# Eagle recurrence followed by a mixture-of-depths MLP on one core: the per-batch second part rescheduled, and the tables and first keys of the start-up rebuilt

## The chip, the cores and the metric

The kernel runs on one core of a Trainium2 chip. The metric is device time in microseconds (us) of one execution, as the median of the timed runs; before the change it is 264.77 us (three runs, 262.55 to 264.99).

## What is computed

The first part is a linear recurrence with decay, for 4 batches, 8 heads, 768 tokens and head width 48, all float32:

```
for t in range(S):
    cur = einsum('bhd,bhe->bhde', u * k[t], v[t])
    y[t] = einsum('bhd,bhde->bhe', r[t], state + cur)
    state = w * state + einsum('bhd,bhe->bhde', k[t], v[t])
```

The heads are laid side by side (8 x 48 = 384 channels) and each batch goes through the second part: every token gets a score, the 128 tokens with the highest scores of the batch go through a two-layer MLP (384 to 1024 to 384), weighted by a sigmoid of the score, and all other rows pass unchanged:

```
scores = x @ w_gate
top_idx = the 128 tokens of the batch with the highest scores
h = maximum(x[b, top_idx] @ w1, 0);  ye = h @ w2
out[b, top_idx] = x[b, top_idx] + sigmoid(scores)[:, None] * ye
```

## The kernel before

**Units.** A unit is 128 tokens of one batch with all 8 heads: 6 units in a batch (NC), 24 in all (NU). Inside a unit there are two chunks of 64 tokens. The order of instructions is written by hand (a manual schedule): each engine executes its own in the order in which the program issues them, so the place of a call in the loop is its place in the queues of all the engines that it uses.

**Tables, before the loop.** `wp` holds the powers w^(2^i) (L123 to L125), `up` and `dn` are rising and falling powers made by doubling (L131 to L142). `kt` (L144 to L147) scales keys, `tr` (L153 to L155) scales receptances; each takes one RECIPROCAL of 128x128. `kt` is transposed on the tensor engine into `wk` (L148 to L152), which scales the keys in their loaded layout. Masks and identity come from an int32 iota on POOL.

**One unit n, in the order of the loop (L459 to L489).** `load(n+4)` puts three transfers on SP's queue. `inner(n)`: 32 instructions at L237 (scores of keys and receptances) and 32 at L244 (key by value), into the one PSUM tile `rp`. `masked(n)` (L250, DVE) copies the causal part of `rp` into `AT[n]`. `state(n, 0)`: `g` on DVE (L255), then four scalings `z` on ACT (L258). `turn(n+1)`: eight transposes on the tensor engine (L216, L219) and the copy `kh` on ACT (L221); `turned(n+1)`: `rh` on DVE (L226); `bonus_sum(n+1)`: `du` on DVE (L206). POOL gets `scaled(n+2)` (`kw`, L196), `diagonal(n+1)` (`at`, L210) and `bonus(n+2)` (`rk`, `rku`, L200, L202). Then `outer(n-1)`: 64 instructions into `y` and `yx` (L272 to L284) and two copies `e` on ACT (L289); `state(n, 1)`; `finish(n-1)`: `x` (L297) and the scores `scr` (L298) on DVE, and the store of the unit.

**The second part of batch b** is hung on the ends of later units by `plan` (L432): with n = 6(b+1), unit n gets `scores_along` (six transposes at L318, two copies `srow` at L319), units n+1 and n+2 get three `compare` each (L326 `gt`, L328 equality), unit n+2 also `rank` (L333 to L341), `pick` (`oh` L350, L353, `idx` L357) and `fetch` (gather of the chosen rows, POOL, L365), unit n+3 `chosen` (transposes L381, copy `xt` L383), `gates` (L388, L391) and the first half of `hidden` (24 instructions at L399), n+4 its second half, n+5 all of `expert` (16 at L408) and `leave` (`ot` L414, scatter on POOL L416). For the last batch all of them come after the loop, in this order. PSUM tiles named `m` (two buffers) serve all of the second part.

**Start.** Before the loop the order is `scaled(0)`, `tables()` (POOL memsets of `rpads` 2 to 4, `zt`, `es`), `bonus(0)`, `bonus_sum(0)`, `turn(0)`, `turned(0)`, `load(2)`, `load(3)`, `scaled(1)`, `diagonal(0)`, `bonus(1)`. `rpads` and `kws` are cleared whole by POOL memsets.

Of the kernel before, what the change touches and what calls it, by code (L numbers as in the profile page):

```python
# [17 lines left out]
def kernel(  # L18
# [71 lines left out]
    for i in range(2):  # L90
        nc.gpsimd.memset(rpads[i], 0.0)
# [17 lines left out]
    jp = const.tile([128, 128], I32)  # L109
    nc.gpsimd.iota(jp, pattern=[[1, 128]], base=0, channel_multiplier=-1)  # L110
# [18 lines left out]


    up = const.tile([128, NP, MID + 1], F32)  # L131
    dn = const.tile([128, NP, MID + 1], F32)
    nc.vector.memset(up[:, :, 0:1], 1.0)
    nc.vector.memset(dn[:, :, MID : MID + 1], 1.0)
    h = 1
    for i in range(NW):
        n = min(h, MID + 1 - h)
        if n > 0:
            nc.vector.tensor_mul(dn[:, :, MID + 1 - h - n : MID + 1 - h],
                                 dn[:, :, MID + 1 - n : MID + 1], power(i, n))  # L140
            nc.vector.tensor_mul(up[:, :, h : h + n], up[:, :, :n], power(i, n))
        h *= 2  # L142
# [70 lines left out]
    def turn(n):  # L213
        pk = psum.tile([128, NP, T], F32, name="pk")
        for hp in range(NP):
            nc.tensor.transpose(pk[:, hp, :], kws[n % 3][:, 2 * hp : 2 * hp + 2, :], ident)  # L216
# [310 lines left out]
```

## Time and profile before

| what | value |
|---|---|
| median of the timed runs | 264.77 us (262.55 to 264.99) |
| the profiled execution's own time | 261.97 us |
| its span, first to last instruction | 260.2 us |
| mean granted clock of the tensor engine, share of 2.4 GHz | 0.821 |
| busy: PE / DVE / ACT / POOL | 178.9 / 127.8 / 85.4 / 114.1 us |

The span is what the views of the trace cover; the time of an execution is 1.77 us longer in the profiled one. An engine's busy share is an average over the start, 24 units and the tail, and no engine is busy throughout, so the limits are read unit by unit. The start of `masked(n)` on DVE serves as the mark of unit n below.

### The profile page before, as it was taken

Reading aid. Unit: us, or ns where it says so; the run is one execution under the profiler, and the core shown is the slowest. Engines: PE = TensorE matmul, PEld = TensorE weight load, DVE = VectorE, ACT = ScalarE, POOL = GpSimd, SP = SyncE. Lnnn points to the kernel's source line nnn. Section 1 sums busy time; section 2 is a strip of 40 time slices with the busy share of each in tenths; the row PEclk is TensorE's granted clock in tenths of the full one; section 3 lists DMA queues with packets and bytes.
Section 4 is the critical chain, followed back from the end, with each engine's and each line's share of the span. In section 5 each row is a group of like instructions: output and inputs, shape, how many; then the busy total and the mean of one; then the engine's idle time right before and its main releaser. Section 6 shows DMA issues by size and latency. Waiting matters only on the chain.

```text
span 260.2 us, 8407 instructions
## 1 busy us (share of the span) xinstructions
PE 178.9 (69%) x3608; PEld 153.8 (59%) x3608; DVE 127.8 (49%) x340; ACT 85.4 (33%) x274; POOL 114.1 (44%) x131
## 2 busy tenths in 40 slices
PE   0347958779609799959509799959229799721991
PEld 0236847759508698649408698659128797411970
DVE  4835765573884235353983245256873153282000
ACT  1003654552242545063232345064313253100110
POOL 4397995594443616464343526474345110101001
PEclk9999997995955799995955799988955599955699
DMA  7899498986741505532741505543001001101000
GB/s 140 133 175 130 113 373 214 193 198 138 151 95 33 121 5 123 121 99 58 149 96 33 123 7 124 119 123 92 3 33 30 33 3 46 49 33 30 0 0 30
DMA packets 81428, 24.52 MB, mean 94 GB/s; under 512 B 76272, under 2 KB 80624, under 8 KB 81392
## 3 DMA queue, kind: packets, MB, share of 16 engines
q1 hardware_dynamic: 79776, 22.03, 39.1%
q0 software_dynamic: 512, 1.57, 1.9%
q10 hardware_dynamic: 1104, 0.40, 0.8%
q8 instruction: 28, 0.46, 0.7%
q14 instruction: 8, 0.07, 0.1%
HBM read 18.48 MB, written 5.51 MB: 92 GB/s over the span
## 4 chain that ended last, share of the span: by engine, by line
PE 51%; DVE 19%; issue 11%; ACT 9%; DMA 4%; POOL 2%; SPq 1%; POOLq 0%; DVEq 0%; ACTq 0%
PE m L399 8%; PE y L272 8%; PE m L408 6%; PE rp L237 6%; PE pk L216 6%; PE rp L244 5%; DVE gt L326 5%; PE pr L219 5%; ACT e L289 4%; ACT z L258 3%; DVE scr L328 3%; DVE scr L298 3%; PE y L281 3%; DMA kin<-in_k_dram 3%; DVE x L297 3%
## 5 line engine op out<-in xcount | busy, mean ns | idle before, releaser
L258 ACT ACTIVATE z<-g,wp 128x48 f32<-128x48 f32 x176 | 44.5, 323 | 89.8 <-DVE g L255 89.3
L210 POOL TENSOR_TENSOR at<-dia,du 128x512 f32<-128x512 f32 x24 | 25.0, 1042 | 72.5 <-DVE du L206 72.4
L272 PE MATMUL y<-vin,at 64*64 64x48 f32 x768 | 42.2, 239 | 1.8 <-issue 1.8
L250 DVE COPY_PREDICATED at<-mask,rp 128x512 f32<-128x512 uint32 x24 | 17.6, 731 | 48.7 <-PE rp L244 36.6
L272 PEld LDWEIGHTS y<-vin,at 64*64 64x64 f32 x768 | 35.6, 153 | 7.5 <-issue 5.8
L284 PE MATMUL yx<-z,rh 48*64 48x48 f32 x352 | 33.1, 251 | 3.2 <-issue 3.2
L281 PE MATMUL y<-z,rh 48*64 48x48 f32 x352 | 30.6, 233 | 0.0
L297 DVE TENSOR_TENSOR x<-y,e 128x384 f32<-128x384 f32 x24 | 13.4, 558 | 33.8 <-ACT e L289 33.8
L196 POOL TENSOR_TENSOR kw<-kin,wk 128x384 f32<-128x384 f32 x24 | 25.2, 1052 | 10.3 <-DVE wk L152 7.5
L399 PE MATMUL m<-xt,w 128*128 128x128 f32 x192 | 29.2, 322 | 0.0
L399 PEld LDWEIGHTS m<-xt,w 128*128 128x128 f32 x192 | 28.2, 236 | 0.2
L202 POOL TENSOR_TENSOR rku<-rk,ub 128x384 f32<-128x384 f32 x24 | 26.8, 1115 | 1.9
L237 PE MATMUL rp<-rh,kh 48*64 48x64 f32 x768 | 20.5, 255 | 7.1 <-DVE rh L226 3.7
L281 PEld LDWEIGHTS y<-z,rh 48*64 48x64 f32 x352 | 22.5, 150 | 2.8 <-issue 2.8
L200 POOL TENSOR_TENSOR rk<-rpad,kin 128x384 f32<-128x384 f32 x24 | 24.0, 1002 | 0.2 <-DMA rpad<-in_r_dram 0.2
L237 PEld LDWEIGHTS rp<-rh,kh 48*64 48x64 f32 x768 | 17.0, 162 | 10.8 <-issue 5.9
L289 ACT COPY e<-yx 64x192 f32<-64x192 f32 x48 | 15.0, 313 | 23.5 <-PE y L281 15.8
L408 PE MATMUL m<-w,ht 128*128 128x384 f32 x64 | 21.6, 491 | 0.0
L216 PE MATMUL pk<-ident,kw 128*128 128x128 f32 x96 | 20.3, 347 | 1.8 <-POOL kw L196 1.8
L336 PE MATMUL m<-ones,gt 128*128 128x1 bf16 x60 | 4.6, 169 | 23.8 <-DVE gt L326 23.8
L284 PEld LDWEIGHTS yx<-z,rh 48*64 48x64 f32 x352 | 20.6, 143 | 0.6 <-issue 0.6
L244 PE MATMUL rp<-vin,kw 64*64 64x48 f32 x704 | 20.2, 247 | 0.3
(81 smaller groups left out, 288.3 us busy)
## 6 DMA issues: line engine op xcount, KB each, us to landing
kin<-in_k_dram SPq DMA_DIRECT2D x24, 192.0 KB, 4.0
rpad<-in_r_dram SPq DMA_DIRECT2D x24, 192.0 KB, 4.1
vin<-in_v_dram SPq DMA_DIRECT2D x24, 192.0 KB, 3.5
out_dram<-x SPq DMA_DIRECT2D x24, 192.0 KB, 2.0
w<-in_moe_w_dram SPq DMA_DIRECT2D x2, 1536.0 KB, 10.4
ub<-in_u_dram ACTq DMA_DIRECT2D x1, 192.0 KB, 4.8
wg<-in_moe_w_gate_dram ACTq DMA_DIRECT2D x1, 192.0 KB, 5.4
xr<-out_dram,idx POOLq DMA_INDIRECT x4, 3.2
```

The source lines that it names most:

```text
L196: nc.gpsimd.tensor_mul(kws[n % 3][:, :, :D], KIN[n], wk)
L202: nc.gpsimd.tensor_mul(RKU[n], rk, ub)
L216: nc.tensor.transpose(pk[:, hp, :], kws[n % 3][:, 2 * hp : 2 * hp + 2, :], ident)
L237: nc.tensor.matmul(out=rp[ts, i, hp * C : (hp + 1) * C], lhsT=KH[n][rows, hp, ts], rhs=RH[n][rows, hp, ts], start=True, stop=True)
L244: nc.tensor.matmul(out=rp[i * PAD : (i + 1) * PAD, c, NP * C + hp * D : NP * C + (hp + 1) * D], lhsT=kws[n % 3][ts, 2 * hp + i, :], rhs=VI ...
L258: nc.scalar.activation(to[:, hp, :], g[:, hp, :], AF.Copy, scale=wc[:, hp : hp + 1])
L272: nc.tensor.matmul(out=y[ts, 2 * hp + i, :], lhsT=AT[n][ts, i * NP + hp, :], rhs=VIN[n][ts, 2 * hp + i, :], start=(hp == 0 and i == 0), st ...
L281: nc.tensor.matmul(out=y[ts, 2 * hp + i, :], lhsT=RH[n][rows, hp, ts], rhs=z[rows, hp, :], start=False, stop=True, skip_group_check=True)
L284: nc.tensor.matmul(out=yx[ts, hp, :], lhsT=RH[n][rows, hp, ts], rhs=z[rows, hp, :], start=True, stop=True)
L289: nc.scalar.copy(e[ts, :, 1 - c, :], yx[ts])
L399: nc.tensor.matmul(out=ph[:, f, :], lhsT=w1[:, d, (f0 + f) * 128 : (f0 + f + 1) * 128], rhs=XT[b, z][:, d, :], start=(d == 0), stop=(d == ...
L408: nc.tensor.matmul(out=pe[:, :Dm], lhsT=HT[b, z][:, f, :], rhs=w2[:, f, :], start=(f == 0), stop=(f == FB - 1))
```

## The change

The second part is cut into smaller steps that run one unit after the data which they read. `work_at(n, "turn")` runs steps after `bonus(n+2)` and ahead of `outer(n-1)`, `work_at(n, "end")` at the unit's end. `scores_along` moves to unit n+1, the compares to the ends of n+1 to n+3 (short ones first), `rank` and the new `match` (the `oh` half of `pick`) to n+4, `pick` and `fetch` to n+5, `chosen`, `gates` and the MLP to n+7 and after, two MLP parts to a place (`hidden` and `expert` now take two blocks at a call). For batch 2 the MLP, and for batch 3 what needs its last two units, come after the loop, interleaved; batch 3's first four units are compared in unit 23. In the start, unit 0's keys are transposed unscaled from a padded tile `k0` and scaled by `kt` on leaving PSUM (DVE), `wk` is made by `key_table` with copies on ACT, the two RECIPROCALs of 128x128 become one of 128x4 and two multiplications, memsets clear only the padding, the iota is float32, and `tables()` moves behind `bonus(1)`.

```diff
+    k0 = const.tile([128, H, PAD], F32)
...
-        KIN[n] = work.tile([128, H, D], F32, name="kin", bufs=NIN)
+        KIN[n] = work.tile([128, H, D], F32, name="kin", bufs=NIN) if n else k0[:, :, :D]
...
-    for i in range(2):
-        nc.gpsimd.memset(rpads[i], 0.0)
+    for x in [k0] + rpads[:2]:
+        nc.gpsimd.memset(x[:, :, D:], 0.0)
...
-    jp = const.tile([128, 128], I32)
+    jp = const.tile([128, 128], F32)
...
-        nc.gpsimd.memset(kws[i], 0.0)
+        nc.gpsimd.memset(kws[i][:, :, D:], 0.0)
...
     for i in range(NW - 1):
         nc.vector.tensor_mul(wp[:, i + 1, :], wp[:, i, :], wp[:, i, :])
+        h = 1 << i
+        if h < MID:
+            nc.vector.tensor_mul(dn[:, :, MID - 2 * h : MID - h], dn[:, :, MID - h :], power(i, h))
+            nc.vector.tensor_mul(up[:, :, h : 2 * h], up[:, :, :h], power(i, h))
+    back = const.tile([128, NP], F32)
+    nc.vector.reciprocal(back, wp[:, MID.bit_length() - 1, :])
+    back = back[:, :, None].to_broadcast([128, NP, MID])
+    nc.vector.tensor_mul(kt[:, :, 0, MID:], dn, back)
+    nc.vector.tensor_mul(tr[:, :, :MID], up, back)
...
-    nc.vector.reciprocal(kt[:, :, 0, MID:], up[:, :, 1:])
-    nc.vector.tensor_copy(kt[:, :, 1, :], kt[:, :, 0, :])
...
-    nc.vector.tensor_copy(wk, p.rearrange("s p (i d) -> s (p i) d", i=2)[:, :, :D])
...
-    nc.vector.reciprocal(tr[:, :, :MID], dn[:, :, :MID])
+    def key_table():
+        nc.scalar.copy(kt[:, :, 1, :], kt[:, :, 0, :])
+        p = psum.tile([128, NP, 128], F32, name="m", bufs=2)
+        for hp in range(NP):
+            nc.tensor.transpose(p[:, hp, :], kt[:, hp, :, :], ident)
+        nc.scalar.copy(wk, p.rearrange("s p (i d) -> s (p i) d", i=2)[:, :, :D])
...
-            nc.gpsimd.memset(rpads[i], 0.0)
+            nc.gpsimd.memset(rpads[i][:, :, D:], 0.0)
...
-        nc.scalar.copy(KH[n], pk)
+        if keys is not None:
+            nc.vector.tensor_mul(KH[n].rearrange("d p (c t) -> d p c t", c=2),
+                                 pk.rearrange("d p (c t) -> d p c t", c=2),
+                                 kt[:, :, 0:1, :].to_broadcast([128, NP, 2, C]))
+        else:
+            nc.scalar.copy(KH[n], pk)
...
-    def compare(b, c):
+    def compare(b, c, first, last):
         s = sc[b][:, c : c + 1]
...
+        lo = max(c, first)
+        nc.vector.tensor_scalar(GT[b][:, c, lo:last, :], SR[b][:, lo:last, :], s, None, op0=OP.is_gt, op1=OP.add,
+                                accum_out=RS[b][-1][:, c : c + 1])
+        if first <= c:
+            nc.vector.scalar_tensor_tensor(scr[:, :128], SR[b][:, c, :], s, earlier, op0=OP.is_equal, op1=OP.mult,
+                                           accum_out=ES[b][:, c : c + 1])
+    def count(b):
+        q = ES[b]
+        for rs in RS[b]:
+            to = work.tile([128, NC], F32, name="q", bufs=4)
+            nc.vector.tensor_add(to, rs, q)
+            q = to
+        QQ[b] = q
...
-        ph = psum.tile([128, 4, 128], F32, name="m", bufs=2)
-        for f in range(4):
+        if f0 % 4 == 0:
+            PH[b, z] = psum.tile([128, 4, 128], F32, name="m", bufs=2)
+        ph = PH[b, z]
+        for f in range(f0, f0 + 2):
...
-        nc.scalar.activation(HT[b, z][:, f0 : f0 + 4, :], ph, AF.Relu)
+        if f0 % 4 == 2:
+            nc.scalar.activation(HT[b, z][:, f0 - 2 : f0 + 2, :], ph, AF.Relu)
...
+    def mlp(b, z):
+        for f0 in range(0, FB, 2):
+            yield hidden, (b, z, f0)
+        for f0 in range(0, FB, 2):
+            yield expert, (b, z, f0)
+        yield leave, (b, z)
     def plan(b):
         n = (b + 1) * NC
...
+        step(n + 1, "turn", scores_along, b, 0, NC)
+        for c in range(NC):
+            step(n + 1 + c // 2, "end", compare, b, NC - 1 - c, 0, NC)
+        step(n + 3, "end", count, b)
+        step(n + 4, "turn", rank, b)
         for z in range(NST):
...
+            step(n + 4, "end", match, b, z)
+            step(n + 5, "turn", pick, b, z)
+            step(n + 5, "turn", fetch, b, z)
+        if n + 6 < NU:
+            for z in range(NST):
+                step(n + 7, "turn", chosen, b, z)
+                step(n + 7, "turn", gates, b, z)
+            parts = [p for z in range(NST) for p in mlp(b, z)]
+            per = -(-len(parts) // 8)
+            for i, (f, a) in enumerate(parts):
+                step(n + 7 + i // per // 2, ("turn", "end")[i // per % 2], f, *a)
...
+    last = B - 1
+    known = NC - 2
+    step(NU - 1, "turn", scores_along, last, 0, known)
+    for c in range(known):
+        step(NU - 1, "end", compare, last, c, 0, known)
...
-    scaled(0)
-    tables()
     bonus(0)
-    bonus_sum(0)
-    pr = turn(0)
+    pr = turn(0, k0)
+    key_table()
     turned(0, pr)
     load(2)
     load(3)
+    scaled(0)
     scaled(1)
+    bonus_sum(0)
     diagonal(0)
     bonus(1)
+    tables()
...
+        work_at(n, "turn")
         if n:
             outer(n - 1)
...
-        for f, a in fill.get(n, []):
-            f(*a)
+        work_at(n, "end")
...
     outer(NU - 1)
     finish(NU - 1)
...
+    rest = []
+    for z in range(NST):
+        chosen(last - 1, z)
+        gates(last - 1, z)
+        rest += mlp(last - 1, z)
...
+    some(2)
+    scores_along(last, known, NC)
+    for c in range(NC):
+        compare(last, c, known, NC)
+    count(last)
+    some(2)
+    rank(last)
+    for z in range(NST):
+        match(last, z)
+    some(2)
+    for z in range(NST):
+        pick(last, z)
+        fetch(last, z)
+    some(len(rest))
+    for z in range(NST):
+        chosen(last, z)
+        gates(last, z)
+        for f, a in mlp(last, z):
+            f(*a)
```

`some(k)` takes the next k parts of batch 2's MLP (`rest`).

## Rows read from the trace of the kernel before

**Rows 1.** Busy time by stretch (PE, PEld, DVE, ACT, POOL), clock, DMA share, GB/s.

```profile
30.52:35.04 4.52, 3.54 (x137) 3.27 (x136) 3.67 (x11) 3.13 (x11) 4.17 (x5) 1.00 1.00 331
25.13:53.22 28.09, 21.99 (x671) 19.84 (x671) 17.90 (x38) 14.84 (x51) 21.23 (x24) 0.94 0.79 216
53.22:216.91 163.69, 122.73 (x2562) 107.37 (x2561) 85.42 (x222) 61.20 (x198) 74.35 (x77) 0.78 0.37 84
216.91:260.20 43.29, 25.14 (x240) 18.87 (x234) 11.22 (x38) 4.96 (x14) 3.15 (x5) 0.79 0.07 24
```

**Rows 2.** Timeline of DVE, end of unit 2 and mark of unit 3.

```profile
33.72 0.56 DVE L297 TENSOR_TENSOR x<-y,e 128x384 f32<-128x384 f32 x1 [0.80 <-ACT e L289]
34.31 0.80 DVE L298 SCALAR_TENSOR_TENSOR scr<-x,wg 128x384 f32<-128x384 f32 x1
35.04 0.73 DVE L250 COPY_PREDICATED at<-mask,rp 128x512 f32<-128x512 uint32 x1
```

**Rows 3.** Timeline of ACT in the same unit.

```profile
32.55 0.59 ACT L221 COPY kh<-pk 128x512 f32<-128x512 f32 x1
33.03 0.65 ACT L289 COPY e<-yx 64x192 f32<-64x192 f32 x2
```

**Rows 4.** Busy time of a unit at the lower clock, same columns as rows 1.

```profile
58.36:64.57 6.21, 6.21 (x135) 5.79 (x138) 2.39 (x5) 1.85 (x6) 2.37 (x4) 0.50 0.71 152
```

**Rows 5.** Chain of waits in the tail: start, length, what.

```profile
230.20 0.80 DVE gt L326 x2
231.00 0.27 DVE scr L328 x2
...
233.02 0.40 DVE gt L326 x2
...
234.74 0.97 DVE oh L350
...
236.55 3.06 DMA xr<-out_dram,idx
```

**Rows 6.** Groups of instructions by form: the score copies on ACT.

```profile
L319 ACT COPY srow<-m 128x512 f32<-128x512 f32 x4 | 2.3, 586 | 0.1
L319 ACT COPY srow<-m 128x256 f32<-128x256 f32 x4 | 1.5, 373 | 1.7 <-PE m L318 1.6
```

**Rows 7.** Timeline of PE: the MLP of batch 1.

```profile
146.04 0.97 PE L388 MATMUL m<-wgc,xt 128*128 128x1 f32 x6 [1.89 <-ACT xt L383]
146.88 4.41 PE L399 MATMUL m<-xt,w 128*128 128x128 f32 x24
...
154.85 2.94 PE L399 MATMUL m<-xt,w 128*128 128x128 f32 x24
...
161.34 5.43 PE L408 MATMUL m<-w,ht 128*128 128x384 f32 x16
```

**Rows 8.** Timeline of the start, all engines.

```profile
7.72 0.94 DVE L146 RECIPROCAL kt<-up 128x128 f32<-128x128 f32 x1
...
9.04 1.11 PE L151 MATMUL m<-ident,kt 128*128 128x128 f32 x4 [9.04 <-DVE kt L147]
...
10.90 0.99 POOL L196 TENSOR_TENSOR kw<-kin,wk 128x384 f32<-128x384 f32 x1 [7.49 <-DVE wk L152]
...
11.66 2.59 DVE L160 TENSOR_SCALAR mask<-jc 128x64 f32<-128x64 int32 x1
...
13.23 0.26 POOL L177 MEMSET zt<- 128x192 f32 x1
...
13.43 0.78 POOL L179 MEMSET e<- 128x384 f32 x2
...
20.31 0.35 DVE L255 TENSOR_TENSOR g<-rp,zt 128x192 f32<-128x192 f32 x1
...
23.05 1.13 PE L237 MATMUL rp<-rh,kh 48*64 48x64 f32 x32 [1.60 <-DVE g L255]
```

**Rows 9.** Timeline of the end, last MLP's result.

```profile
254.81 0.62 DVE L414 SCALAR_TENSOR_TENSOR ot<-m,gate,xr 128x384 f32<-128x384 f32 x1 [18.54 <-PE m L408]
```

More of the change, by code (lines that the diff above doesn't have):

```diff
@@ L125 @@
         nc.vector.tensor_mul(wp[:, i + 1, :], wp[:, i, :], wp[:, i, :])
-    def power(i, n):
-        return wp[:, i, :, None].to_broadcast([128, NP, n])
[L131 to L142, printed above, removed]
@@ L305, in finish, with scores_along @@
         stores.setdefault(b, []).append(st)
-    SR, GT, RS, ES, QQ, XR, XT, IDX, GA, HT, PE = {}, {}, {}, {}, {}, {}, {}, {}, {}, {}, {}
+    SR, GT, RS, ES, QQ, XR, XT, IDX, GA, HT, PH, PE, OH = ({} for _ in range(13))
     spacer = const.tile([1, 1], F32)
     out_rows = out.rearrange("b s d -> (b s) d")
-    def scores_along(b):
-        SR[b] = work.tile([128, NC, 128], F32, name="srow")
-        for c0 in range(0, NC, 4):
-            c1 = min(c0 + 4, NC)
+    def scores_along(b, first, last):
+        if first == 0:
+            SR[b] = work.tile([128, NC, 128], F32, name="srow")
+            GT[b] = work.tile([128, NC, NC, 128], BF16, name="gt", bufs=1)
+            ES[b] = work.tile([128, NC], F32, name="eq")
+            RS[b] = []
+        for c0 in range(first, last, 4):
+            c1 = min(c0 + 4, last)
             p = psum.tile([128, 4, 128], F32, name="m", bufs=2)
@@ L406, in expert @@
         pe = PE[b, z]
-        for f in range(f0, f0 + 4):
+        for f in range(f0, f0 + 2):
             nc.tensor.matmul(out=pe[:, :Dm], lhsT=HT[b, z][:, f, :], rhs=w2[:, f, :],
@@ L430, with step, work_at @@
     fill = {}
+    def step(n, where, f, *a):
+        fill.setdefault((n, where), []).append((f, a))
+    def mlp(b, z):
[4 more added lines that the diff above has]
+        yield leave, (b, z)
     def plan(b):
         n = (b + 1) * NC
-        steps = [(n, scores_along, (b,))]
-        steps += [(n + 1 + c // 3, compare, (b, c)) for c in range(NC)]
-        steps.append((n + 2, rank, (b,)))
-        for z in range(NST):
-            steps += [(n + 2, pick, (b, z)), (n + 2, fetch, (b, z)), (n + 3, chosen, (b, z)), (n + 3, gates, (b, z))]
-            steps += [(n + 3 + f0 // 4, hidden, (b, z, f0)) for f0 in range(0, FB, 4)]
-            steps += [(n + 5 + f0 // 8, expert, (b, z, f0)) for f0 in range(0, FB, 4)]
-            steps += [(n + 5, leave, (b, z))]
-        for m, f, a in steps:
-            fill.setdefault(min(m, NU), []).append((f, a))
-    for b in range(B):
-        plan(b)
-    scaled(0)
-    tables()
+        step(n + 1, "turn", scores_along, b, 0, NC)
[3 more added lines that the diff above has]
+        step(n + 4, "turn", rank, b)
+        for z in range(NST):
+            step(n + 4, "end", match, b, z)
[9 more added lines that the diff above has]
+                step(n + 7 + i // per // 2, ("turn", "end")[i // per % 2], f, *a)
+    for b in range(B - 2, -1, -1):
+        plan(b)
+    last = B - 1
[3 more added lines that the diff above has]
+        step(NU - 1, "end", compare, last, c, 0, known)
+    def work_at(n, where):
+        for f, a in fill.get((n, where), []):
+            f(*a)
     bonus(0)
-    bonus_sum(0)
-    pr = turn(0)
+    pr = turn(0, k0)
+    key_table()
     turned(0, pr)
```

69 lines of the change are left out of this document (34 added, 35 removed).

## The prediction

> **What bounds the kernel now.** I read the busy times by stretch first, with the start of masked(n) on DVE as mark, because no engine is busy throughout. From mark 1 to mark 6, which is almost without second part, five units take 28.09 us; from mark 6 to mark 23, where the second parts of batches 0 to 2 lie, seventeen take 163.69; from mark 23 to the end 43.29 [rows 1]. So a unit costs 5.6 without and 9.6 with the second part, and PE is busy for only 122.73 of the 163.69.
>
> A unit in the open takes 4.52 us at 2.4 GHz, with PE busy for 3.54 of it [rows 1]. The timelines of DVE and ACT say what closes it: `x` waits for the `e` copies, `scr` ends as the next mark begins (34.31 + 0.80 against 35.04), and `e` comes behind `kh` in ACT's queue [rows 2, 3]. The loop is at, g, z, kh, e, x, scr, at; with 0.73, 0.59, 0.65, 0.56 and 0.73 to 0.80 for the ones in the rows, some 1.2 are left for g and z. Two rules follow. What is put on DVE behind `scr`, or on ACT between `kh` and `e`, lengthens a unit by its full duration. PE has about 1.0 us to spare; beyond that it binds (of its 3.54 I count 1.1 for inner, 1.0 for turn, 1.4 for outer). At 1.2 GHz PE is itself the bound: 6.21 us, all of it busy [rows 4].
>
> **The start.** Now the chain runs through the RECIPROCAL of `kt` (0.94), its copy, four transposes (9.04 to 10.15), `wk`, `kw` at 10.90 and POOL's memsets, which end at 14.21 [rows 8]; the first `g` comes at 20.31 and unit 1 begins on PE at 23.05. After the change what stands ahead of the RECIPROCAL (7.72) is shorter by two small multiplications and a copy (0.3), and a four-column reciprocal and one multiplication take its place (0.4, by its 0.94 for 128 columns an upper estimate): `kt` is ready at 7.9 instead of 8.7. Then ACT's copy (no row of this one; the 128x256 copy from PSUM takes 0.37 [rows 6]; 0.4) 8.3, transposes 1.11 9.4, the second ACT copy (0.55, between those of 256 and 512 columns) 10.0. POOL then has five operations of about 1.05 (kw of units 0 and 1, at 0, rk and rku 1; 0.99 for the first [rows 8]): 15.3. bonus(0) lies ahead of them in the 7.49 in which POOL now waits. Behind them comes tables(): three small memsets (at most 0.26 each by the `zt` row; 0.5 together) and `zt` itself: 16.1. That is what becomes late: the first `g` reads `zt`, so it starts at 16.2, whatever masked(0) does before, and on DVE `rh` and `du` of unit 1 are queued behind it, on ACT z and kh. From `g` to unit 1 on PE it was 2.74; with the transposes of unit 1 long done only z (1.0), kh (0.6) and latencies stay, 2.0: 18.2 instead of 23.05, **-4.8 us**. Upper end -6.0 (`kt` by 7.3, the interleaved doubling having no stall; the POOL operations as short as 0.99). Lower end -2.7: bonus(0) now runs beside the table building, two operations of 1.05 each, and if each stops DVE entirely, `kt` is 2.1 late. That engines do stop each other is in the rows: the `mask` operation on DVE stands for 2.59 us and ends at 14.25, right after POOL's last memset at 14.21 [rows 8]. I take none of the 2.1, because these rows are a one-input DVE operation against writes, and keep it in the range.
>
> The Trainium skill, "SBUF — State Buffer", section "Who interferes with whom", speaks against the change here: a DVE instruction with two SBUF inputs contends with a POOL instruction that reads SBUF, and the later one blocks until the first is through. The table multiplications are of that kind and so are rk and rku. By that rule the gain is the lower end, and the sum below 2.1 us longer; no row of the start shows the pair.
>
> Mark 1 so moves from 25.13 to 20.3; marks 1 to 6 keep their 28.1 (nothing in them changes; SP's loads are issued as early or earlier, `load(2)` no longer waits for the whole memset, and a third transfer still waits for outer(n-1)), so mark 6 is at 48.4.
>
> **The loop.** Removed are PE's waits in order: for the scores just made, for the compares ahead of rank, for `oh`, for the gathered rows; each is now read a unit later. The transfers keep their order on SP's queue and are hidden: 84 GB/s over 163.69 us become 108 over 127, where marks 1 to 6 had 216 [rows 1]. The work itself stays, by the two rules. A `gt` of 640 columns takes 0.80 in its chain, one of 256 0.40, so 0.13 for each 128 columns; each equality 0.27; `oh` 0.97 [rows 5]. At 2.4 GHz:
> - unit 6: nothing, 4.5.
> - unit 7: two srow copies between kh and e, 0.59 + 0.37 [rows 6], compares of 128 and 256 columns 0.27 + 0.40 + 0.54: 4.5 + 2.1 = 6.6.
> - unit 8: 0.53 + 0.67 + 0.54: 6.2.
> - unit 9: 0.80 + 0.93 + 0.54 and count 0.2: 7.0.
> - unit 10: rank's add and `oh`: 5.6. Rank's sixteen small matmuls fit in PE's spare 1.0.
> - unit 11: idx 0.2: 4.7. The gather adds 1.0 on POOL, which is busy 4.17 of 4.52 [rows 1]: it starts the next units up to 0.8 late, and what it makes is needed more than a unit later.
> - unit 12: 4.5.
>
> The MLP is nominally spread, but nine parts by two fill two and a half units: 13, 14 and `leave` in 15. Unit 13: in PE's order scores_along of the next batch, then `chosen`, must wait for kh and both srow copies before `xt`, and outer(12) with e, x and scr is queued behind on PE; with 1.0 for at and g, 1.0 for z, 0.6 kh, 1.0 srow, 0.3 transposes and 0.5 `xt` the gates start at 4.3 to 4.4 after the mark, take 0.97, then 24 hidden 2.94, outer 1.4, 24 hidden 2.94 and inner 1.1 [rows 7]: 13.6. Its compares lie beside PE. Unit 14: turn 1.0, expert 5.43 in two halves, outer 1.4, inner 1.1: 9.0, the compares again covered. Unit 15: `ot` falls into DVE's wait for `e`; compares and count as in unit 9: 7.0. Units 16 to 18: 5.6, 4.7, 4.5. Units 19 to 22 like 13 to 16: 35.2.
>
> Sum of marks 6 to 23: 39.1 + 44.4 + 35.2 = **118.7 us at 2.4 GHz**.
>
> **The clock.** After the stretches without matmuls the trace has 1.2 GHz: hidden's first half takes 4.41, the second 2.94 [rows 7]. A compare unit of 7.0 leaves PE idle for 3.4 of it, so I expect the fall to stay, shorter. Within compare units it costs nearly nothing: 6.21 is below 7.0. After them I charge one open unit per batch with 6.21 - 4.52 = 1.7 and a little, 2.0, and the first half of hidden 1.47: 3 x 2.0 + 2 x 1.47, less as batch 2 is cut short, 8.3. Loop: **127 us** against 163.69. Ends: 0 and 20 (below).
>
> **The tail.** From mark 23: scr(22) at 4.5, four compares 2.95, x and scr of unit 23 1.4: 8.9. Beside this PE does outer(23), chosen, gates and half of batch 2's hidden, to 10.3: it holds the last two score transposes. Copy 11.3, compares of the last two units' columns (five of 0.40, one 0.27, two equalities) 14.1, count and rank 14.9, `oh` 15.9. PE then is still in half of expert to 17.3; pick and idx 17.9, gather 3.06 and 0.3: 21.2; chosen, xt, gates 2.3: 23.5; hidden 5.9, expert 5.4: 34.8; from `ot` to the span's end 5.4 as now (254.81 to 260.2 [rows 9]): 40.2, with 1.4 for a cold half of hidden 41.6 against 43.29. So the tail gives little: batch 2's MLP now lies in it.
>
> **Sum.** 20.3 + 28.1 + 127 + 41.6 = 217.0 us of span, with the 1.77 outside it 218.8 against 261.97 of the profiled execution. The median of the timed runs lies 1.07% above that execution; the same factor gives **221 us**.
>
> **Rivals.**
> 1. The clock stays at 2.4 GHz: without the 8.3 and 1.4 the median is 211. For it: PE's idle stretches become short. Against: 3.4 us idle in units 9, 15, 21.
> 2. The clock falls in every batch and returns late: eight open or nearly open units at 6.21 (five by 1.7, three by 1.2: 12) instead of the 6 charged for them, and both halves of hidden cold (2 x 1.47 more), some PE waits left: 231. By the Trainium skill, "TensorE: Matmul & The Clock Gate", Part 4, transposes don't count as activity like matmuls do; if so this rival gains, as a unit's eight transposes would count as idle. The cold unit in the trace came back with its transposes in it [rows 4], which does not decide it.
> 3. Slower than before: the steps in small pieces keep PE busy too thinly and it stays at 1.2 GHz throughout. Units then cost 6.2, the MLPs twice: open units +12, compare units +3, two MLPs +27, tail +17, early units +4, from the 207 of the hot sum: 270 of span, 275 median. It decides only where more than about 85% of the time is spent at 1.2. Against: after one full unit the trace has 2.4 again, and PE's share rises.
> 4. The change doesn't do what it says, the MLP isn't spread: true as worked out, and priced; PE binds there anyway.
>
> **Chances.** Forecast (214 to 227) 0.58; rival 1 0.14; rival 2 0.23; rival 3 0.02; something that leaves no change 0.03. Range 207 to 239, from rival 1 with the full gain of the start and 3 us less of waits to rival 2 with its lower end and 5 us more of waits. Faster by over 1% (about what a measurement tells here) 0.95, within 0.03, slower 0.02.
>
> **What would show it.** Right: unit 1's L237 near 18, first `g` waiting for POOL's `zt`; no wait of L336 on `gt` inside the loop; units 13 and 14 near 14 and 9; mark 23 near 175; compares directly lengthening units. Wrong: units of 6 us without steps (clock), DVE's table multiplications stretched beside rk (start), `masked` waiting for POOL (its queue late), or outer(n-1) held by `xt` in more than units 13 and 19.

## The result and the profile after

The changed kernel takes 226.06 us (median of 4 runs, 222.41 to 227.53), the kernel before, measured beside it, 263.66 (4 runs, 260.39 to 264.99): ratio 0.8553, with an interval of 0.83 to 0.8807. Ratios here are taken over the faster runs of each kernel, and the profiled execution of the changed one, with 227.53 us, is one of its slower ones. The prediction was 221 us, its range 207 to 239. From group to group of runs the kernel before takes other times (medians and single runs from 253.8 to 264.8 us), so each kernel below is compared with those that ran beside it, or stretch by stretch through its trace.

The span of the profiled execution is 225.73 us, the mean granted clock 0.856 of 2.4 GHz instead of 0.821. First the busy time by stretch, between the same marks as in [rows 1] (start of masked(n) on DVE, now L251); the columns are PE, PEld, DVE, ACT, POOL, clock, DMA share and GB/s.

```profile
20.73:48.51 27.78, 22.40 (x671) 20.48 (x671) 18.03 (x40) 14.93 (x51) 21.66 (x24) 0.94 0.75 203
48.51:178.54 130.03, 107.57 (x2483) 94.78 (x2481) 85.38 (x221) 59.07 (x194) 73.44 (x75) 0.84 0.48 107
178.54:225.73 47.19, 37.14 (x308) 30.61 (x308) 11.99 (x50) 6.80 (x18) 4.20 (x7) 0.79 0.08 26
```

Against [rows 1] mark 1 is 4.4 us earlier (20.73 for 25.13), marks 1 to 6 are as long as before (27.78 for 28.09), the loop has lost 33.7 (130.03 for 163.69), and the tail has grown by 3.9 (47.19 for 43.29). Together -34.5, the difference of the spans (260.20 to 225.73). DVE's work in the loop is the same, 85.4 us; what went is time in which DVE did nothing. Part of the 33.7 is not saved but moved: batch 2's gates and hidden, which before lay in units 21 and 22, now lie in the tail, where PE's busy time went from 25.14 to 37.14 us.

The start, from the timeline of all engines:

```profile
5.81 1.01 POOL L196 TENSOR_TENSOR rk<-rpad,k 128x384 f32<-128x384 f32 x1 [3.85 <-DMA rpad<-in_r_dram]
5.86 0.98 DVE L141 TENSOR_TENSOR kt<-kt,wp 128x16 f32<-128x16 f32 x1
...
6.94 1.02 POOL L198 TENSOR_TENSOR rku<-rk,ub 128x384 f32<-128x384 f32 x1
7.03 0.98 DVE L142 TENSOR_TENSOR tr<-tr,wp 128x32 f32<-128x32 f32 x1
...
11.04 1.02 POOL L192 TENSOR_TENSOR kw<-k,wk 128x384 f32<-128x384 f32 x1 [3.08 <-ACT wk L157]
...
16.71 0.36 DVE L256 TENSOR_TENSOR g<-rp,zt 128x192 f32<-128x192 f32 x1 [1.91 <-POOL zt L173]
...
18.65 1.13 PE L238 MATMUL rp<-rh,kh 48*64 48x64 f32 x32 [3.54 <-ACT kh L222]
```

The first `g` waits for POOL's `zt`, as predicted; it starts at 16.71 and unit 1 begins on PE at 18.65 (16.2 and 18.2 forecast; in [rows 8] 20.31 and 23.05). Two of DVE's small multiplications last 0.98 us each, and each ends as POOL's operation beside it does: 5.86 + 0.98 = 6.84 beside 5.81 + 1.01 = 6.82, and 8.01 beside 7.96.

In the loop PE's waits for scores, `oh` and gathered rows are gone. These are the sums by waiting line over the whole execution (total us, times, longest):

```profile
PE rp L238 <- ACT kh L222: 13.1, 8, 3.5
PE m L349 <- DVE gt L333: 4.9, 3, 1.8
PE m L398 <- ACT srow L324: 4.6, 2, 2.4
...
PE y L273 <- issue: 3.5, 3, 1.5
```

The largest, inner's wait for `kh`, lies in the loop with 8.0 of its 13.1 us: it is the unit's own loop through DVE and ACT, which the prediction describes. `chosen` (L398) is held by both score copies, as it counted too. But it had expected no wait of `rank` for the compares in the loop, and three are left (L349), 4.9 us in all, where the kernel before has 23.8 at that step. The first, ahead of `outer` in unit 10, costs nothing: that `outer` ends at 77.61, and ACT copies its result only at 78.38, when `kh` is through. PE's timeline of unit 13 from `chosen` on, and of the tail:

```profile
95.66 0.74 PE L398 MATMUL m<-ident,xr 128*128 128x128 f32 x3 [2.41 <-ACT srow L324]
96.97 1.44 PE L405 MATMUL m<-wgc,xt 128*128 128x1 f32 x6 [0.57 <-ACT xt L400]
98.27 5.04 PE L418 MATMUL m<-xt,w 128*128 128x128 f32 x24
...
104.76 2.94 PE L418 MATMUL m<-xt,w 128*128 128x128 f32 x24
...
189.69 5.39 PE L418 MATMUL m<-xt,w 128*128 128x128 f32 x24
...
206.23 0.53 PE L398 MATMUL m<-ident,xr 128*128 128x128 f32 x3 [0.93 <-DMA xr<-out_dram,idx]
...
208.01 7.23 PE L418 MATMUL m<-xt,w 128*128 128x128 f32 x48
```

The same 24 matmuls take 5.04 in unit 13 and 5.39 in the tail, 2.94 where the clock is at 2.4 GHz. By the clock's records it is at 1.2 GHz from 95.9 to 102.7, from 174.4 to 194.9 and from 208.5 to 211.9.

The length of each unit, from mark to mark, against the prediction's (without the 8.3 us for the clock in the loop and the 1.4 in the tail), with a second profile of the same kernel ("again", run later, span 224.65):

| units | predicted | after | again |
|---|---|---|---|
| 6 to 12 | 39.1 | 44.0 | 43.7 |
| 13, 14 | 13.6, 9.0 | 16.4, 9.0 | 16.3, 9.0 |
| 15 to 18 | 7.0, 5.6, 4.7, 4.5 | 8.0, 6.2, 5.6, 4.5 | 8.0, 6.2, 5.6, 4.5 |
| 19, 20 | 13.6, 9.0 | 15.1, 9.0 | 16.7, 9.0 |
| 21, 22 | 7.0, 5.6 | 7.1, 5.1 | 7.1, 5.1 |
| tail | 40.2 | 47.2 | 44.6 |

### The profile page after: what moved, and what is told of

It is laid out like the page before. It is cut to its first block, busy times and chain, and to the rows that moved or that the text cites. A ratio compares the mean times of both kernels' runs of the same rounds, so it can differ in the third digit from the quotient of the medians.

```text
span 225.7 us, 8416 instructions
## 1 busy us (share of the span) xinstructions
PE 176.6 (78%) x3608; PEld 153.5 (68%) x3608; DVE 124.7 (55%) x346; ACT 85.4 (38%) x275; POOL 112.2 (50%) x132
## 3 DMA queue, kind: packets, MB, share of 16 engines
q1 hardware_dynamic: 79776, 22.03, 43.4%
## 4 chain that ended last, share of the span: by engine, by line
PE 47%; issue 19%; DVE 14%; ACT 11%; DMA 4%; POOL 3%; POOLq 1%; ACTq 0%; DVEq 0%
PE y L273 9%; PE m L418 7%; PE pk L212 5%; PE m L428 5%; PE rp L238 5%; ACT z L259 4%; PE pr L215 4%; PE y L282 4%; PE rp L245 4%; ACT e L290 3%; DVE x L298 3%; PE yx L285 3%; ACT kh L222 3%; DVE gt L333 2%; DVE scr L299 2%
## 5 line engine op out<-in xcount | busy, mean ns | idle before, releaser
L273 PE MATMUL y<-vin,at 64*64 64x48 f32 x768 | 43.2, 242 | 5.0 <-issue 3.5
L273 PEld LDWEIGHTS y<-vin,at 64*64 64x64 f32 x768 | 36.4, 156 | 10.1 <-issue 8.4
L282 PE MATMUL y<-z,rh 48*64 48x48 f32 x352 | 31.4, 240 | 1.4 <-issue 1.4
L238 PE MATMUL rp<-rh,kh 48*64 48x64 f32 x768 | 20.9, 256 | 14.3 <-ACT kh L222 13.1
L418 PE MATMUL m<-xt,w 128*128 128x128 f32 x192 | 30.9, 335 | 0.5 <-ACT ht L421 0.5
L418 PEld LDWEIGHTS m<-xt,w 128*128 128x128 f32 x192 | 29.8, 248 | 0.8 <-ACT ht L421 0.7
L198 POOL TENSOR_TENSOR rku<-rk,ub 128x384 f32<-128x384 f32 x24 | 26.0, 1084 | 1.9
L282 PEld LDWEIGHTS y<-z,rh 48*64 48x64 f32 x352 | 23.3, 157 | 0.0
L196 POOL TENSOR_TENSOR rk<-rpad,kin 128x384 f32<-128x384 f32 x23 | 23.1, 1003 | 0.0
L251 DVE COPY_PREDICATED at<-mask,rp 128x512 f32<-128x512 uint32 x24 | 17.6, 732 | 7.8 <-PE rp L245 4.6
L333 DVE TENSOR_SCALAR_CACHE_REDUCE gt<-srow,sc 128x256 bf16<-128x256 f32 (+5 forms) x28 | 16.7, 607 | 7.1 <-ACT srow L324 7.1
L299 DVE SCALAR_TENSOR_TENSOR scr<-x,wg 128x384 f32<-128x384 f32 x24 | 18.8, 785 | 0.8
```

The costliest lines, as they stand in the source:

```text
L198: nc.gpsimd.tensor_mul(RKU[n], rk, ub)
L238: nc.tensor.matmul(out=rp[ts, i, hp * C : (hp + 1) * C], lhsT=KH[n][rows, hp, ts], rhs=RH[n][rows, hp, ts], start=True, stop=True)
L273: nc.tensor.matmul(out=y[ts, 2 * hp + i, :], lhsT=AT[n][ts, i * NP + hp, :], rhs=VIN[n][ts, 2 * hp + i, :], start=(hp == 0 and i == 0), st ...
L282: nc.tensor.matmul(out=y[ts, 2 * hp + i, :], lhsT=RH[n][rows, hp, ts], rhs=z[rows, hp, :], start=False, stop=True, skip_group_check=True)
L299: nc.vector.scalar_tensor_tensor(scr, x, 1.0, wg, op0=OP.mult, op1=OP.mult, accum_out=sc[b][:, c : c + 1])
L418: nc.tensor.matmul(out=ph[:, f % 4, :], lhsT=w1[:, d, f * 128 : (f + 1) * 128], rhs=XT[b, z][:, d, :], start=(d == 0), stop=(d == KD - 1))
```

## The experiments

**The two halves of the change, apart.** First the changed kernel with the start of before, its table building, memsets and integer iota included; of the edit this is the order of the calls:

```diff
-    bonus(0)
-    pr = turn(0, k0)
-    key_table()
+    scaled(0)
+    tables()
+    bonus(0)
+    bonus_sum(0)
+    pr = turn(0)
...
```

> The changed loop and tail with the start of before. My theory (the start and the loop are separate gains, the start worth the 4.4 us by which mark 1 moved, 25.13 to 20.73): mark 1 near 25.1, the span 4 to 5 us above that of the changed kernel (225.7), so near 230, and units 7 to 22 as long as there. Rival (the earlier start only moves the wait to the weights' load, so that the loop makes the whole gain): span within 1.5 us of 225.7.

It took 232.26 us in one run (before beside it: 257.96). Span 230.49, 4.8 more than the changed kernel; mark 1 at 25.51.

Second, the kernel before with the new start alone. Against the changed kernel, the second part is planned as before:

```diff
+        steps = [(n, scores_along, (b,))]
+        steps += [(n + 1 + c // 3, compare, (b, c)) for c in range(NC)]
+        steps.append((n + 2, rank, (b,)))
...
-        step(n + 1, "turn", scores_along, b, 0, NC)
...
```

> The changed start with the loop of before. My theory: first g on DVE near 16.7, mark 1 near 20.7 and the span about 4.4 us below that of before (260.2), 255 to 257, with the same waits of PE for scores, compares and gathered rows in the loop. Rival (the start's gain is given back in the first units, by the loads): marks 6 within 1.5 us of before's 53.22.

256.48 us in one run (before beside it: 257.96); span 254.71, 5.5 below that of before. Mark 1 came at 20.70 and mark 6 at 47.37; from there on it is the kernel before: loop 164.14, tail 43.20 [rows 1]. PE's waits are those that the change takes away, here by line:

```profile
PE m L337 <- DVE gt L327: 24.8, 16, 5.0
PE m L319 <- DVE scr L299: 9.5, 4, 2.7
PE m L354 <- DVE oh L351: 8.4, 4, 2.1
PE m L389 <- ACT xt L384: 5.2, 4, 1.5
```

These four lines hold 47.9 us, tail included. By the spans of the profiles the halves add up: 29.7 us for the loop and tail alone, 5.5 for the start alone, 35.2 together against 34.5 measured. The two times side by side differ by only 1.5 us for the start alone, but one run each can't decide that, as the kernel before varies by more from run to run; the marks can: mark 1 is 4.4 to 4.8 us earlier by the new start, with either loop.

**What bounds the new start.** The same start with the tables made first:

```diff
+    tables()
     bonus(0)
...
     bonus(1)
-    tables()
```

> The changed kernel with the POOL memsets of tables() ahead of bonus(0), where POOL waits for the first receptances from 1.96 to 5.81. My theory (the first g waits for zt alone, 1.91 us by the trace): g follows masked(0) near 14.8, and mark 1 comes 1.5 to 2 us earlier, at 18.8 to 19.2. Rival (the loads or the transposes of unit 1 are as late): mark 1 stays at 20.7 within 0.4.

219.51 us, span 217.74. `g` no longer waits for `zt`, and mark 1 is at 19.00 instead of 20.73:

```profile
14.54 0.36 DVE L256 TENSOR_TENSOR g<-rp,zt 128x192 f32<-128x192 f32 x1
```

So the order on POOL's queue was the end of the start, as predicted, and 1.7 us were left there. The other 6 us of this span lie in the units, mostly before mark 13 and in the tail, where profiles of one kernel differ as well; nothing shows them to be a gain of this edit.

Next, POOL is held back by an operation of one column on `kt`, so that `rk` and `rku` of unit 0 come behind the table building:

```diff
+    kdep = const.tile([128, 1], F32)
+    nc.gpsimd.tensor_mul(kdep, kt[:, 0, 0, MID : MID + 1], kt[:, 0, 0, MID : MID + 1])
     bonus(0)
```

> The changed kernel with a one-column POOL operation on kt ahead of bonus(0), so that rk and rku of unit 0 start when the table building on DVE is through. My theory (two table multiplications that stand for 0.98 us beside rk and rku are held by POOL's reads): both take 0.2 us, the key table is ready 1.5 us earlier, kw of unit 0 starts near 9.5 instead of 11.04, and mark 1 comes 1.2 to 1.6 us earlier. Rival (they were late for another reason, their own length or the weights' column): kw still at 11.0, or later by the moved bonus(0).

221.93 us, span 220.15, mark 1 at 19.20. The two stretched multiplications are short (0.17 and 0.18), and `wk` (8.88 for 10.48) and `kw` come earlier by about as much:

```profile
5.88 0.17 DVE L141 TENSOR_TENSOR kt<-kt,wp 128x16 f32<-128x16 f32 x1
...
9.51 1.01 POOL L192 TENSOR_TENSOR kw<-k,wk 128x384 f32<-128x384 f32 x1
```

The contention is real: 0.98 became 0.17 and 0.18, and `kw` began at 9.51 instead of 11.04. It cost 1.5 us of the start. The Trainium skill, "SBUF — State Buffer", section "Who interferes with whom", says that a DVE instruction with two SBUF inputs contends with a POOL instruction that reads SBUF, for ports that are an exclusive lock; these rows agree.

**The MLP in the loop.** Two kernels and the changed kernel again, for what the rest is compared with:

> The changed kernel itself once more, as the reference of this set: 222 to 228 us, with the tensor engine at 1.2 GHz again around marks 22 and 23 and in the first hidden half of the tail.

226.14 us (4 runs, 223.78 to 226.88), ratio 0.8596 [0.8536, 0.8656]. Its tail is 2.57 us shorter than in the first profile, and two groups of matmuls say why: PE's timeline has them as

```profile
191.19 4.46 PE L418 MATMUL m<-xt,w 128*128 128x128 f32 x24
...
208.56 5.60 PE L418 MATMUL m<-xt,w 128*128 128x128 f32 x48
```

where the first profile has 5.39 and 7.23. The differences, 0.93 and 1.63, are the 2.57 but for 0.01. So what the two tails differ by is the clock. In the loop units 6, 10 and 19 differ by 1.1 to 1.6 us as well.

First `chosen` is taken a place earlier, behind unit n+6, so that it isn't held by the next batch's score copies (the planning loop is turned round, so that the gates and the first half of hidden come ahead of the score transposes):

```diff
-                step(n + 7, "turn", chosen, b, z)
+                step(n + 6, "end", chosen, b, z)
...
-    for b in range(B - 2, -1, -1):
+    for b in range(B - 1):
```

> The changed kernel with chosen at the end of the unit before the MLP, and in the MLP's first unit gates and hidden ahead of the next batch's score transposes. My theory (in units 13 and 19 PE stands about 3 us behind kh, both score copies and xt, and the first half of hidden is then at 1.2 GHz): units 13 and 19 fall from 16.41 and 15.14 to 10.5 to 12 us, the time by 7 to 10 us less up to 1 us in units 12 and 18, which now may wait for the gathered rows. Rival (PE's work binds these two units anyway): less than 3 us.

223.78 us (4 runs), ratio 0.8531 [0.8478, 0.8584], which overlaps that of the changed kernel: the expected gain wasn't there. Units 13 and 19 fell to 14.1 and 11.5, but 12 and 18 rose from 4.9 and 4.5 to 8.0 and 7.0. The chosen rows had not landed:

```profile
88.10 0.90 PE L398 MATMUL m<-ident,xr 128*128 128x128 f32 x3 [3.30 <-DMA xr<-out_dram,idx]
```

The wait for the score copies was exchanged for one on the gather of 3.30 us, in the same in-order queue.

Then the MLP with one part to a place instead of two (and `leave` ahead of the next pick):

```diff
-                step(n + 7 + i // per // 2, ("turn", "end")[i // per % 2], f, *a)
+                step(n + 7 + i // 2, ("turn", "end")[i % 2], f, *a)
...
+    for b in range(B - 2):
+        at = fill[(b + 1) * NC + 11, "turn"]
+        at.insert(0, at.pop())
```

> The changed kernel with one MLP part to a place instead of two, so that batches 0 and 1 spread theirs over units 13 to 16 and 19 to 22 (leave a unit later, ahead of the next pick). My theory (in compare units PE idles up to 3 us, which MLP parts could fill, while two parts to a place make PE the bound of two units): units 13 to 16 together fall from 39.6 to 30 to 35 us, the time by 8 to 14 us. Rival (PE binds in sum, or thinner work leaves the clock at 1.2 GHz): within 3 us of the changed kernel.

221.92 us (4 runs), ratio 0.845 [0.8412, 0.8488]: about 4 us better, half of the least that was expected. Units 13 to 16 went from 39.6 to 33.0, as expected, but 19 to 22 only from 37.9 (again) to 34.3, unit 18 rose from 4.5 to 6.8, and the tail was no shorter. Why unit 18 rose is not shown: POOL issues scatter and gather there one behind the other (at 132.43 and 133.75), and PE stands for 0.44 and 0.39 us for nothing that the profile shows.

**Do compares lengthen a unit directly?** The equality operations are left out:

```diff
+            nc.gpsimd.memset(ES[b], 0.0)
...
-        if first <= c:
-            nc.vector.scalar_tensor_tensor(scr[:, :128], SR[b][:, c, :], s, earlier, op0=OP.is_equal, op1=OP.mult,
-                                           accum_out=ES[b][:, c : c + 1])
```

> The changed kernel without the 24 equality operations of compare (ties between scores are then not broken), their sums set to zero. My theory (what stands behind scr on DVE lengthens its unit by its full length): units 7, 8, 9, 15 and 21 shorter by 0.54 each, unit 23 by 1.1, the tail by 0.5, together 4 us. Rival (the compares are hidden in the unit's other chain, by PE at the lower clock): less than 1.5 us.

220.52 us (5 runs), ratio 0.8352 [0.8318, 0.8387]. Units 7, 8 and 9 are 6.26, 5.71 and 6.45 instead of 7.27, 6.52 and 7.00, two equalities less in each: 1.01, 0.81 and 0.55 us, where these took 1.02, 0.81 and 0.54 of DVE's queue in the changed kernel (from one start to the next). Unit 21 is 0.55 shorter, unit 15 only 0.3: without the equality, the small sum behind it is held up instead (1.38 us). These five units make 3.2 of the 5.6 us by which the medians differ; the rest is not followed up. So the compare units carry DVE's queue end to end; in the changed kernel, unit 8:

```profile
66.12 0.80 DVE L299 SCALAR_TENSOR_TENSOR scr<-x,wg 128x384 f32<-128x384 f32 x1
...
66.85 0.60 DVE L333 TENSOR_SCALAR_CACHE_REDUCE gt<-srow,sc 128x384 bf16<-128x384 f32 x1
...
67.38 0.55 DVE L336 SCALAR_TENSOR_TENSOR scr<-srow,sc,earlier 128x128 f32<-128x128 f32 x1
...
68.86 0.73 DVE L251 COPY_PREDICATED at<-mask,rp 128x512 f32<-128x512 uint32 x1
```

**Which neighbour `chosen` should have.** It is put a place later, at the end of unit n+7, behind `outer`, and gates, hidden and expert from n+8 on:

```diff
-                step(n + 7, "turn", chosen, b, z)
-                step(n + 7, "turn", gates, b, z)
+                step(n + 7, "end", chosen, b, z)
+                step(n + 8, "turn", gates, b, z)
...
-                step(n + 7 + i // per // 2, ("turn", "end")[i // per % 2], f, *a)
+                step(n + 8 + i // per // 2, ("turn", "end")[i // per % 2], f, *a)
```

> The changed kernel with chosen at the end of the MLP's first unit and gates, hidden and expert from the next unit on, so that neither the gathered rows nor xt are waited for. My theory (the long units 13 and 19 are PE standing behind kh, the score copies and xt, then hidden at the lower clock): unit 13 near 6.6, unit 14 near 10, unit 15 near 9.6, unit 16 6.2, together 32 to 33 instead of 39.6; the same in 19 to 22 less than 33 instead of 36.3 to 38; the span 11 to 13 us below that of the changed kernel (224.7 in its second profile, 225.7 in its first). Rival (as with chosen early, a wait comes back elsewhere): less than 6 us.

207.92 us in one run (before beside it: 253.81), span 206.14. Units 13 to 16 are 7.3, 8.3, 9.2 and 6.2, 31.0 for 39.6; units 19 to 22 29.3 for 36.3 to 37.9. The loop as a whole, in the columns of the stretches above:

```profile
50.56:162.79 112.23, 96.79 (x2478) 85.34 (x2474) 85.61 (x221) 58.33 (x194) 73.17 (x74) 0.92 0.52 117
```

The same steps on PE's timeline of this kernel:

```profile
95.68 0.55 PE L398 MATMUL m<-ident,xr 128*128 128x128 f32 x3 [0.90 <-ACT srow L324]
...
98.16 0.73 PE L405 MATMUL m<-wgc,xt 128*128 128x1 f32 x6
98.75 2.92 PE L418 MATMUL m<-xt,w 128*128 128x128 f32 x24
...
103.80 2.94 PE L418 MATMUL m<-xt,w 128*128 128x128 f32 x24 [0.59 <-ACT gate L408]
```

The loop is 17.8 us shorter than in the changed kernel, 15.6 of it in units 13 to 16 and 19 to 22. That is more than was expected, and the rows say what is different: gates and both halves of hidden run at 2.4 GHz, which in unit 13 is worth 0.7 and 2.1 us, and PE waits ahead of them for 0.90 instead of 2.41 and 0.57. Between `xt` and the gates lie inner and turn of the next unit, so PE doesn't stand idle there. From mark 6 on the clock is at 1.2 GHz for 28 us instead of 62.

**The tail.** The last scores and compares are put ahead of batch 2's hidden:

```diff
-    some(2)
     scores_along(last, known, NC)
```

> The changed kernel with the last batch's remaining score transposes and compares ahead of batch 2's hidden in the tail, and rank and pick each two MLP parts earlier. My theory (from mark 23 on PE's own work binds, much of it at 1.2 GHz): the gather is issued 4 to 6 us earlier, but the span falls by 1 to 2.5 us only, since batch 2's MLP then lies ahead of batch 3's anyway; mark 23 to the end 43 to 46. Rival (the chain scores, compares, gather binds the tail): mark 23 to the end falls by 5 us or more from 44.6 to 47.2.

222.6 us in one run, span 220.80; the tail 43.82 us, against 47.2 and 44.6. The gather of batch 3 starts 20.9 us after mark 23 (197.92 after 176.98) instead of 24.5 (203.08 after 178.54) or 23.6 (again). PE's timeline:

```profile
197.70 5.43 PE L428 MATMUL m<-w,ht 128*128 128x384 f32 x16 [0.25 <-DVE idx L374]
202.96 0.49 PE L398 MATMUL m<-ident,xr 128*128 128x128 f32 x3
...
204.71 5.60 PE L418 MATMUL m<-xt,w 128*128 128x128 f32 x48
```

`chosen` (L398) now follows batch 2's expert without a wait, where it waited 0.93 for the gathered rows. Against the second profile, whose last hidden also took 5.60, the tail is 0.8 shorter, about that wait. The gather came 2.7 to 3.6 us earlier, not the 4 to 6 expected. Tails with the old order took 43.4 to 47.7 us in nine profiles here, so the 43.82 alone says little; that `chosen` no longer waits says that PE's own work carries the tail, not the chain to the gather.

Then 18 matmuls whose results nobody reads, six in unit 22, six before and six after the last outer:

```diff
+    def keep(k):
+        p = psum.tile([128, 4, 128], F32, name="m", bufs=2)
+        for f in range(k):
+            nc.tensor.matmul(out=p[:, f % 4, :], lhsT=ident, rhs=w1[:, 0, :128], start=True, stop=True)
...
+    step(NU - 2, "turn", keep, 6)
...
+    keep(6)
     outer(NU - 1)
+    keep(6)
```

> The changed kernel with eighteen more matmuls of 128x128 whose results nobody reads: six ahead of the rest in the turn place of unit 22, six before and six after the last outer, where PE waits. My theory (the tail is late because PE was at 1.2 GHz from unit 22 to the end of the first half of hidden): the clock is at 2.4 GHz in that half, it takes 2.9 instead of 5.4 us, and mark 23 to the end is 42 us or less in spite of up to 2 us of added work. Rival (the order of the work makes the tail, not the clock): 44.6 or more.

219.68 us in one run, span 217.90. The tail took 42.15 us, just above the 42 expected. In the changed kernel the stretches of the tail up to the end of the first half of hidden are:

```profile
178.54:184.19 5.65, 4.01 (x74) 3.55 (x75) 1.70 (x7) 2.22 (x7) 1.09 (x2) 0.50 0.13 38
184.19:194.91 10.72, 10.15 (x98) 9.66 (x98) 4.54 (x21) 1.28 (x4) 0.00 (x0) 0.50 0.12 39
```

In this kernel, from mark 23 on:

```profile
175.75:182.76 7.01, 6.86 (x150) 6.26 (x150) 3.24 (x13) 2.22 (x7) 1.09 (x2) 0.76 0.19 61
182.76:188.72 5.96, 5.39 (x49) 5.15 (x47) 2.92 (x15) 1.27 (x4) 0.00 (x0) 1.00 0.11 37
```

and that half itself, on PE's timeline:

```profile
185.96 2.92 PE L423 MATMUL m<-xt,w 128*128 128x128 f32 x24
```

With more work on PE the tail is shorter: the clock is at 1.2 GHz only up to 179.7, and the first half of hidden takes 2.92 instead of 5.39. So the clock is a large part of what made the tail late. It need not be all: six of the unread matmuls also fill a time in which PE had waited 1.50 us (below).

**All that helped, together**: tables first, `bonus(0)` behind `kt`, `chosen` late, the tail's order and the unread matmuls.

> The changed kernel with all that helped: memsets of tables() first, bonus(0) behind the key table, chosen at the end of the MLP's first unit and the rest from the next on, the tail in the other order, and the eighteen unread matmuls. My theory (these are separate terms: start -3.2 by marks, loop -13 to -17, tail -2 to -4 against 44.6): the span 198 to 203, mark 1 near 17.5, mark 23 to the end 41 to 42.5, ratio to the kernel before 0.76 to 0.79. Rival (they share a cause, the clock, so that the gains don't add): span above 205.

202.36 us (6 runs, 201.3 to 203.37; before beside it 255.46), ratio 0.7955 [0.79, 0.801], just above the 0.76 to 0.79 expected; against the fastest of the 11 runs of the kernel before beside it, 249.18, it is 0.81. It beats both kernels. Its stretches, with mark 1 now at 17.55:

```profile
17.55:44.34 26.79, 22.70 (x672) 20.48 (x671) 17.97 (x40) 14.85 (x51) 21.87 (x24) 0.94 0.99 246
44.34:158.90 114.56, 97.17 (x2494) 84.91 (x2492) 87.78 (x221) 58.29 (x194) 74.29 (x75) 0.94 0.55 120
158.90:200.14 41.24, 33.51 (x332) 27.53 (x332) 11.91 (x50) 6.91 (x18) 4.17 (x7) 0.93 0.09 31
```

Against the changed kernel: -3.2 at mark 1, -1.0 to mark 6, -15.5 in the loop, -6.0 in the tail, the -25.6 by which the spans differ.

## Why the prediction was right, and where it was off

The time was 2.3% above the forecast of 221, inside its own 214 to 227. In span 217.0 was forecast and 225.7 measured, 8.7 more. That the time came closer is luck in part: the forecast put 1.07% on top (2.3 us), because the profiled execution of before lay below the median; here it lay above.

- **The start** (20.3 forecast for mark 1, 20.73 measured) was right, with errors that partly cancel. The contention of which I took none cost 1.6 us at `kt`; but without it `kt` would have been ready at 7.24 (6.95 + 0.29, where POOL is held back) and not at 7.9. So `kt` came at 8.84, 0.9 late, and the first `g` 0.5 late. The late link was POOL's `zt`, as the prediction had it: taking it out of the way gave 1.7.
- **Marks 1 to 6** stayed: 27.78 for 28.1, though in the other profiles the same five units take 26.0 to 29.8.
- **The loop's mechanism** was right: with the waits in order gone, a unit costs its DVE loop plus the compares behind `scr`, and the two MLP units are PE's. Units 8, 9, 14, 18, 20 and 21 came within 0.35 us. Leaving the equalities out shortened three compare units by just what they took of DVE's queue, as the rule says.
- **The loop's clock.** 8.3 were charged for it; the loop came out 11.3 above the hot sum (130.0 for 118.7). Units 13 and 19 cost 2.8 and 1.5 more (again: 2.7 and 3.1), for a charge of 1.47 each: hidden's half takes 5.04 and gates 1.44, where the rows of before had 4.41 and 0.97 [rows 7]. Of the open units behind the compares, 11, 12 and 17 cost 0.9, 0.4 and 0.9 more than hot, less than the 2.0 charged for each batch; unit 22 nothing. Rival 2, a clock that returns late, is so partly true; from mark 6 on there are some 62 us at 1.2 GHz, where before had 90. The kernel with `chosen` late shows that it can be had back: there gates and hidden are hot, which is a part of the 15.6 us by which its two MLPs are shorter.
- **DVE beside POOL in the loop** was priced at nothing, and it makes 3.2 of the 11.3. I took 0.27 for each equality and 0.97 for `oh` from the chain of the tail [rows 5], where POOL does nothing. There an equality lasts 0.35 us and `oh` 0.96; in the loop, beside POOL's multiplications, they last up to 1.32 and 1.74:

```profile
80.10 1.20 POOL L198 TENSOR_TENSOR rku<-rk,ub 128x384 f32<-128x384 f32 x1
80.37 1.74 DVE L365 TENSOR_TENSOR oh<-slots,qq 128x768 bf16<-128x768 f32 x1
...
124.49 1.32 DVE L336 SCALAR_TENSOR_TENSOR scr<-srow,sc,earlier 128x128 f32<-128x128 f32 x1
124.65 1.00 POOL L192 TENSOR_TENSOR kw<-kin,wk 128x384 f32<-128x384 f32 x1
```

  By this units 7, 8 and 15 are 0.7, 0.3 and 1.0 longer than forecast and units 10 and 16 0.6 each. It is not the clock: with `chosen` late unit 16 lies at 2.4 GHz, `oh` takes 1.75 there, and the unit 6.19, as here. The rows look like the contention of the start once more, which the forecast kept in its range there and left out in the loop.
- **Unit 6** took 6.56 for 4.5, and this was in no term. PE stops for 1.54 us for nothing that the profile shows, and the clock is at 1.2 GHz from there to 54.9:

```profile
51.16 0.37 PE L273 MATMUL y<-vin,at 64*64 64x48 f32 x5 [1.54 <-issue]
```

  Such stops of 0.4 to 2.9 us come in the first units of every kernel here, before and after, at other places each time. No experiment tried their cause, but the traces point to one. The page of the profile has a DMA queue of the kind "instruction" (q8, with 28 packets and 0.46 MB in the changed kernel). Its packets are of 16 KB; there are 28 in kernels with 7216 instructions on PE and 29 in the two with 7288. Of the 51 stops over 0.3 us in the 14 profiles, 49 end 1.25 to 1.63 us after a packet of this queue has ended (the one above ends at 51.16, after a packet from 48.71 to 49.74). So PE seems to wait there for its own instructions; that is not shown by a change.
- **The tail** is the step that failed in size: 41.6 forecast, 47.2 and 44.6 measured, so that it grew where it was to shrink. I had the first half of hidden end 10.3 after mark 23, with 1.4 on top for its cold half, and `idx` at 17.9. It ended at 16.5 and `idx` at 24.3; from there to the end the forecast held (22.3 hot, 22.9 measured, 21.3 again). What failed is the overlap ahead of `idx`. PE was to do the last outer beside DVE's work; but that outer writes `y`, of which there is one, and waits until `x` of unit 22 has read it:

```profile
184.19 0.52 PE L273 MATMUL y<-vin,at 64*64 64x48 f32 x5 [1.50 <-DVE x L298]
```

  And the clock was at 1.2 GHz from unit 22 to the end of hidden's half, so that both outers and the gates were slow and not that half alone; in the first profile the last hidden lost another 1.63. With the unread matmuls the half ended 13.1 after mark 23, their own time included, and the tail took 42.15, close to the forecast.
- **The other rivals.** 1 and 3 didn't happen: the clock did fall, and its mean rose instead of sinking. Of rival 4, what was worked out holds: the MLP fills two units and isn't spread. On the transposes that rival 2 spoke of, no run decides.
- **The signs.** Unit 1 on PE at 18.65, the wait for `zt`, unit 14 at 9.0 and the compares that lengthen units came as named; unit 13 (16.4 for 14) and mark 23 (178.5 for 175) came late, and `rank` still waits for the compares. One sign of being wrong came too: the table multiplications stretched beside `rk`.

## What to carry to other kernels

In an engine's in-order queue a step should stand behind something that is ready later than its own data, and ahead of something that fills the time until its result is read: putting `chosen` half a unit later, and the MLP a unit, was worth 15 us, half a unit earlier nothing that the runs tell apart. When PE is cut free of waits, read the granted clock for the stretch ahead of each long run of matmuls; the cold half is a term of its own (2.1 to 2.5 us here). Take the price of a DVE operation from a stretch in which POOL does what it will do beside it, not from one where POOL stands still. A gain in the loop can come back in the tail, where the work that was spread must end.

## What the runs showed of the hardware that was not expected

- A multiplication of 16 columns on DVE with both inputs in SBUF took 0.98 us beside POOL's 1.01 us multiplication, and 0.17 without it. An operation that starts while POOL's is under way is held for what is left of that one: `scr` (128x384, two inputs in SBUF) takes 0.80 where POOL's has 0.38 to go (unit 8), 1.08 where it has 0.67 to go (unit 11), and 0.56 in the tail, where POOL does nothing. The equality of 1.32 us was held even by one that started 0.16 us after it. It holds the other way as well: `kw`, 1.00 to 1.02 alone, takes 1.72 where it starts 0.85 before the end of `oh` (unit 10).

```profile
184.08 0.56 DVE L299 SCALAR_TENSOR_TENSOR scr<-x,wg 128x384 f32<-128x384 f32 x1
```

- More work on PE can shorten a stretch: with 18 unread matmuls the first half of hidden took 2.92 us instead of 5.39 and 4.46.
- PE at 1.2 GHz did not return to 2.4 while it worked for 4.01 of 5.65 us and then 10.15 of 10.72 us; it rose at 194.9, as that half of hidden ended. Why not earlier is open.
